# Batch 0 in a new order: sixteen-row loads of the last key and value rows, key sums by pairwise additions, an expert guess on one column

## The chip, the cores and the metric

The kernel runs on one core of a Trainium2 chip. The core has a matrix engine (PE, with its weight loads listed apart as PEld), a vector engine (DVE), a scalar engine (ACT), a general engine (POOL) and a sequencer (SP) that here does little but start DMAs. Each engine runs its own list of instructions in order and waits on semaphores for the others. The metric is the device time of one execution in microseconds (us): the median of the runs.

## The reference, cut to what matters

```python
# attention per batch b (8) and head (8); 576 tokens, head size 64
k_p = k.reshape(B, H, 72, 8, D).mean(axis=3)     # keys and values pooled over 8 rows
v_p = v.reshape(B, H, 72, 8, D).mean(axis=3)
attn = softmax(q @ k_p.T / sqrt(D));  x = attn @ v_p      # x: 4608 tokens x 512
# two-step routing: best of 4 groups, then best of the 4 experts of that group
g_idx = argmax(x @ w_group);  e_idx = argmax(x @ w_expert[g_idx])
out = g_w * e_w * (relu(x @ w1[g_idx, e_idx]) @ w2[g_idx, e_idx])
```

Each token goes through one of 16 experts, with w1 of 512 x 1024 and w2 of 1024 x 512.

## The kernel before, in words

**Stages.** For each batch the kernel has an attention part (class Att) and an expert part (class Moe). The expert part takes all 576 tokens of a batch through one expert, the one that most of its tokens choose ("main expert"); the tokens of other experts are done at the very end by a loop (class Left). While the expert part of batch b runs on PE, the attention of batch b+1 is worked in between its matmuls.

**Batch 0 is special.** Nothing runs beside its attention, and its expert's weights can't be loaded before the expert is known. So the kernel guesses the expert: guess_x and guess_e route the mean of the values, as if each token attended to all keys alike. guess_e ends with a number (tile me) that SP loads into a register, and the loads of the expert's weights (tile sw) take their address from it. Any guess gives a right output, since tokens of other experts go to the loop.

**Names.** u is a half of the heads (0 or 1), c a piece of 128 tokens (the last of 64), g a pair of heads.

- load_k, load_v: 512 KB of keys or values for 128 of the 144 pooled rows of a pair (tile kv). load_r: the other 16 rows of each pair (tile rem), keys in partitions 96 to 127, values in 64 to 95.
- kr, vr, rr: the sums over 8 rows, from kv into kp or vp, and from rem into rp. On DVE it is one reduction; on POOL it is fold, three additions of 512, 256 and 128 elements.
- kb, kt: masks the key sums on ACT and transposes them on PE. qt: transposes a piece of q on PE. sc: scores. mx, sb, su_, nm: maximum, subtraction and exponential, sum and reciprocal, and normalization (nm on DVE with "v", on POOL with "p"). px_, pm: transposed probabilities; pxd, pmd: their low parts. av: attention output, avd: its low part (tile xt). rt, route, count, gates, keep_x: routing and what hangs on it.
- vmain, vrem: value operands for av, partly on POOL.
- m.load m:j loads quarter j of w1 (m=1) or w2 (m=2); m.split makes a high part on ACT (a cast) and a low part on POOL, or on DVE with "v". m.up f:h is twelve matmuls of the first layer (slice f, token half h), which need both parts of quarter f // 2; m.upd its low part on DVE. m.down is the second layer.
- t.warm: matmuls on a constant, whose result nobody reads.

**What sets the order.** The strings START (up to the first m.up), FIRST (batch 0's expert part and batch 1's attention), STEADY and LAST list the pieces; the letters are a for batch 0's attention, n and x for the next two, m for the expert part, w for the next one's. A piece issues all its instructions and DMAs, on whatever engines, at its place. For START all five engines keep the string's order, for FIRST only PE, SP and DVE do; ACT and POOL are then ordered by the framework's scheduler, as are instructions that must wait for a tile to be given up (the loads load_qb of batch 1's q stand later on SP than in the string). Loads are issued by SP, one queue, in order.

Of the kernel before, what the change touches and what calls it, by code (L numbers as in the profile page):

```python
# [46 lines left out]
a.avd:2:256:320 m.split:2:0 n.vr:0 a.av:1:256:320 a.avd:1:256:320 a.av:3:256:320 n.load_v:1 m.load:2:2 n.qb:0 m.up:5:0 a.avd:3:256:320 n.rr
a.rt:256:320 n.kb m.upd:5:0 a.route t.warm:3 m.upd:2:0 x.load_k:0 n.rcopy n.kt m.up:6:0 n.sc:0 m.up:7:0 n.mx:0 n.vr:1:p n.qb:1 n.sb:0
m.up:0:1 m.upd:6:0 n.sc:1 m.upd:7:0 m.split:2:1:p n.su_:0 n.mx:1 n.nm:0:p n.qb:2 m.up:1:1 m.upd:0:1 n.sb:1 a.count n.px_:0 m.up:2:1 a.gates
m.upd:1:1 n.su_:1 n.sc:2 n.nm:1:p x.load_k:1 n.qb:3 n.vmain x.load_r:k x.load_r:v n.pxd:0 n.vrem n.mx:2 m.up:3:1 m.up:4:1 n.px_:1 n.pm:0  # L50
m.upd:2:1 a.keep_x n.sb:2 m.up:5:1 m.load:2:3 n.pmd:0 m.upd:3:1 x.load_qb:3 n.pm:1 x.load_qb:2 n.sc:3 n.pxd:1 n.su_:2 m.upd:5:1 n.pmd:1
m.up:6:1 n.nm:2:p x.load_v:0 m.up:7:1 n.mx:3 n.pm:2 n.sb:3 m.split:2:2:p m.upd:4:1 n.qb:4 n.px_:2 n.sc:4 n.su_:3 m.upd:7:1 n.pxd:2 n.nm:3:p
n.px_:3 n.mx:4 n.pmd:2 n.av:1:0:256 m.split:2:3:p n.sb:4 n.pm:3 m.upd:6:1 n.pxd:3 n.pmd:3 m.down:0 n.su_:4 n.nm:4:p n.av:2:0:256
n.av:0:0:256 m.down:1 n.avd:2:0:256 n.avd:0:0:256 n.avd:1:0:256 n.av:3:0:256 x.load_qb:1 n.px_:4 n.pm:4 n.pxd:4 n.pmd:4 x.kr:0 n.avd:3:0:256
x.load_qb:0 m.down:2 n.av:0:256:320 n.avd:0:256:320 n.rt:0:256 n.av:1:256:320 n.avd:1:256:320 n.av:2:256:320 n.avd:2:256:320 n.av:3:256:320
x.load_v:1 n.avd:3:256:320 x.rr n.rt:256:320 x.qb:1 m.down:3 x.rcopy x.kr:1 n.route m.down:4 x.kb m.down:5 m.down:6 x.qb:0 n.main_expert
m.down:7 n.gates w.load:1:0 m.down:8 x.kt x.vr:1:v w.split:1:0:v m.down:9 x.sc:0 x.vrem x.mx:0 w.load:2:1 w.load:1:1 w.load:1:3 m.down:10
x.sb:0 x.su_:0 w.load:1:2 x.nm:0:v x.vr:0:p m.down:11 n.keep_x m.down:12 x.vmain w.split:1:1:p m.down:13 w.load:2:0
# [817 lines left out]
```

## Time and profile before

| | us |
|---|---|
| median of 3 runs | 615.87 (615.83 to 618.83) |
| the profiled execution | 614.83 |
| its span, first to last instruction | 612.7 |

| engine | busy us | share of the span |
|---|---|---|
| PE | 589.0 | 96% |
| PEld | 525.6 | 86% |
| DVE | 404.8 | 66% |
| ACT | 281.8 | 46% |
| POOL | 253.8 | 41% |

The page cuts the span into 40 slices of some 15.3 us. PE is at 9 tenths in all slices but the first and the third (6 tenths each) and the last (6); the granted PE clock is at full speed but in the first and the fourth slices. DVE is at 8 or 9 tenths in the fifth to the eighth slice. The slices of batch 0 are the first eight or so: the first matmul of its expert part starts at 39.24 us, that of batch 1's at 133.8 us.

Reading the profile: a row of the timeline gives the start and length of one instruction, or of several alike, and in brackets how long the engine stood idle before and what ended the wait. Lengths of matmuls overlap, since PE is pipelined: starts tell more than lengths.

### The profile page before, as it was taken

What the parts mean: (1) busy time and instruction counts of PE and PEld (TensorE: products, weight loads), DVE (VectorE), ACT (ScalarE), POOL (GpSimd) and SP (SyncE); (2) the same over time, 40 slices, a digit from 0 to 9 for tenths busy, and PEclk for the clock granted to TensorE, in tenths of its full rate; (3) what the DMA queues carried; (4) which work ended last, traced back from release to release, by engine and by line L of the source; (5) the groups of instructions that cost most, each with busy time, mean ns of one, the idle gap of its engine ahead of it and who ended that gap; (6) DMA issues with size and microseconds to landing.
All of it is one profiled execution on the core that took longest, in us unless ns stands there. A gap on an engine that the chain in (4) does not pass through costs nothing.

```text
span 612.7 us, 10857 instructions
## 1 busy us (share of the span) xinstructions
PE 589.0 (96%) x3841; PEld 525.6 (86%) x3841; DVE 404.8 (66%) x1000; ACT 281.8 (46%) x585; POOL 253.8 (41%) x255
## 2 busy tenths in 40 slices
PE   6969999999999999999999999999999999999996
PEld 5858887789988999789988998789978998899874
DVE  4886998879774696548774696549673783347231
ACT  3544635366444653555344653455434643243121
POOL 3034546056423663275424663275424662253100
PEclk8998999999999999999999999999999999999999
DMA  6476415255517542454517552484517200541911
GB/s 186 101 243 113 157 36 113 77 200 200 112 52 242 171 83 75 138 186 124 110 49 242 173 88 68 148 347 115 112 39 245 92 1 2 177 176 26 381 68 40
DMA packets 118761, 81.30 MB, mean 133 GB/s; under 512 B 76327, under 2 KB 95271, under 8 KB 118321
## 3 DMA queue, kind: packets, MB, share of 16 engines
q1 hardware_dynamic: 112656, 70.83, 39.4%
q10 hardware_dynamic: 6016, 9.70, 4.4%
q8 instruction: 32, 0.52, 0.4%
q14 instruction: 25, 0.20, 0.1%
q0 software_dynamic: 32, 0.04, 0.0%
HBM read 75.01 MB, written 28.38 MB: 169 GB/s over the span
## 4 chain that ended last, share of the span: by engine, by line
PE 78%; DVE 13%; DMA 3%; ACT 2%; issue 2%; SPq 1%; POOL 0%; DVEq 0%; POOLq 0%
PE mm L532 28%; PE mm L553 26%; PE sc L291 5%; PE tp L358 5%; PE mm L563 5%; DVE kp L208 3%; PE tp L343 2%; DMA kv<-in_v_dram 2%; DMA sw<-in_moe_w_dram 1%; DVE ht L539 1%; PE tp L331 1%; ACT kb L226 1%; PE tp L371 1%; DVE px L320 1%; DVE xt L363 1%
## 5 line engine op out<-in xcount | busy, mean ns | idle before, releaser
L532 PE MATMUL mm<-xt,w 128*128 128x256 f32 (+1 forms) x1536 | 224.5, 301 | 3.8 <-DVE ht L539 1.6
L532 PEld LDWEIGHTS mm<-xt,w 128*128 128x128 f32 x1536 | 208.7, 190 | 7.1 <-issue 1.7
L553 PE MATMUL mm<-w,ht 128*128 128x512 f32 x768 | 187.7, 396 | 0.0
L518 POOL TENSOR_TENSOR w<-sw,w 128x1024 fp32r<-128x1024 f32 x54 | 131.7, 2456 | 95.2 <-ACT w L517 90.9
L553 PEld LDWEIGHTS mm<-w,ht 128*128 128x128 f32 x768 | 140.8, 188 | 29.3 <-issue 0.8
L534 ACT ACTIVATE ht<-mm 128x256 fp32r<-128x256 f32 (+1 forms) x128 | 52.2, 408 | 112.2 <-PE mm L532 110.8
L539 DVE SCALAR_TENSOR_TENSOR ht<-mm,ht 128x256 fp32r<-128x256 f32 (+1 forms) x192 | 60.5, 344 | 35.0 <-ACT ht L534 34.9
L517 ACT CAST w<-sw 128x1024 fp32r<-128x1024 f32 x64 | 65.5, 1048 | 23.2 <-DMA sw<-in_moe_w_dram 13.4
L320 POOL TENSOR_TENSOR px<-p,su 128x96 f32<-128x96 f32 (+1 forms) x72 | 24.5, 360 | 96.3 <-DVE su L312 53.2
L298 DVE TENSOR_REDUCE mx<-sc 128x8 f32<-128x576 f32 (+1 forms) x40 | 29.9, 748 | 36.5 <-PE sc L291 36.5
L291 PE MATMUL sc<-kT,qT 128*128 128x144 f32 (+1 forms) x320 | 47.4, 292 | 0.0
L291 PEld LDWEIGHTS sc<-kT,qT 128*128 128x128 f32 (+1 forms) x320 | 42.6, 184 | 2.3 <-issue 1.6
L324 POOL TENSOR_TENSOR p<-p,su 128x576 f32<-128x576 f32 (+1 forms) x36 | 41.4, 1149 | 2.8
L558 ACT ACTIVATE y<-mm,gm 128x512 f32<-128x512 f32 x32 | 21.9, 684 | 36.8 <-PE mm L553 36.7
L305 ACT ACTIVATE p<-p 128x576 f32<-128x576 f32 (+1 forms) x40 | 27.3, 683 | 21.8 <-DVE p L304 21.7
L310 DVE TENSOR_REDUCE su<-p 128x8 f32<-128x576 f32 (+1 forms) x40 | 29.9, 746 | 8.9 <-ACT p L305 7.9
L569 DVE TENSOR_TENSOR y<-mm,y 64x512 f32<-64x512 f32 x8 | 5.5, 682 | 44.7 <-ACT y L568 44.7
L363 DVE TENSOR_TENSOR xt<-tp,xt 128x320 fp32r<-128x320 f32 (+2 forms) x68 | 29.3, 437 | 7.9 <-ACT xt L359 6.2
L359 ACT CAST xt<-tp 128x320 fp32r<-128x320 f32 (+2 forms) x68 | 26.1, 384 | 17.1 <-PE tp L358 15.1
L208 DVE TENSOR_REDUCE kp<-kv 128x128 f32<-128x1024 f32 x16 | 31.0, 1971 | 2.7 <-DMA kv<-in_k_dram 2.7
L304 DVE TENSOR_TENSOR p<-sc,mx 128x576 f32<-128x576 f32 (+1 forms) x40 | 30.2, 754 | 3.3
L230 POOL TENSOR_TENSOR kv<-kv 128x512 f32<-128x512 f32 x13 | 16.8, 1292 | 32.8 <-DMA kv<-in_v_dram 32.3
(206 smaller groups left out, 739.0 us busy)
## 6 DMA issues: line engine op xcount, KB each, us to landing
sw<-in_moe_w_dram SPq DMA_DIRECT2D x72, 512.0 KB
xscr<-xt SPq DMA_DIRECT2D x8, 2304.0 KB
kv<-in_k_dram SPq DMA_DIRECT2D x16, 512.0 KB
kv<-in_v_dram SPq DMA_DIRECT2D x16, 512.0 KB
out_dram<-y ACTq DMA_DIRECT2D x32, 256.0 KB
q<-in_q_dram SPq DMA_DIRECT2D x112, 72.0 KB
kv<-in_moe_w_dram SPq DMA_DIRECT2D x6, 512.0 KB
ph<-xscr SPq DMA_DIRECT2D x2, 1152.0 KB
```

Of the source, the lines that this page charges most:

```text
L208: red(out=s.kp[:, 2 * u:2 * u + 2, :], in_=s.k[u].rearrange("p g (j d) -> p g d j", j=8), axis=AX.X, op=ALU.add)
L291: nc.tensor.matmul(ps[0:n, g // 2, 144 * (g % 2):144 * (g % 2) + 144], lhsT=s.qT[c][:, g, 0:n], rhs=s.kT[:, g, :], start=(g % 2 == 0), sto ...
L324: eng.tensor_tensor(out=p[0:n], in0=p[0:n], in1=su[0:n].unsqueeze(3).broadcast_to([n, 2, 4, SP]), op=ALU.mult)
L358: nc.tensor.matmul(ps[:, 0:n], lhsT=flat(l[:, g]), rhs=r, start=(i == 0), stop=(i == len(ops) - 1))
L363: tt(out=s.xt[:, 1, g, sl], in0=s.ta[g][:, 0:n], in1=s.xt[:, 0, g, sl].bitcast(F32), op=ALU.subtract)
L517: nc.scalar.copy(out=wh, in_=raw)
L518: (nc.vector if eng == "v" else nc.gpsimd).tensor_tensor(out=wl, in0=raw, in1=wh.bitcast(F32), op=ALU.subtract)
L532: nc.tensor.matmul(ps[:, 0:n], lhsT=l[:, kc, fs], rhs=xt[:, r, kc, sl], start=(kc == 0 and i == 0), stop=(kc == 3 and i == 2))
L534: nc.scalar.activation(out=ht[:, sl], in_=ps[:, 0:n], func=AF.Relu)
L539: stt(out=ht[:, at:at + hi - lo], in0=ps[:, lo - o:hi - o], scalar=0.0, in1=ht[:, lo:hi].bitcast(F32), op0=ALU.max, op1=ALU.subtract)
L553: nc.tensor.matmul(ps, lhsT=s.ht[f][:, 640 * l + o:640 * l + o + 128], rhs=s.w[2, f // 2][r][:, f % 2, :], start=(i == 0), stop=(i == 23))
L563: nc.tensor.matmul(ps, lhsT=s.ht[f][:, 512:640], rhs=s.w[2, f // 2][r][:, f % 2, :], start=(i == 0), stop=(i == 15))
```

## The change

The strings START and FIRST list all pieces of batch 0 in another order. Beside that:

- load_r uses two DMAs of 16 partitions and both halves of the heads, where it used two of 32 partitions and one half each.
- A helper "total" does all the sums: "r" is the reduction on DVE, "v" three additions on DVE, "p" three on POOL. In batch 0 the second key half and the rows of rem are summed by three additions on DVE, both value halves by the reduction; batch 1's second key half goes to POOL, as both its value halves do.
- The first and second halves of batch 0's keys are put into two tiles of pool wp ("w"), so the kv tiles are free for other loads.
- The guess multiplies the value sums by single columns of sel: twelve matmuls with one column, where the columns had been copied 128 times first. The copying (guess) is gone; the one column is spread when it is copied out of PSUM.
- The router's weights (load_wr) are loaded through ACT's queue, no longer SP's.
- 38 matmuls of t.warm are left, of 56: 35 stand before the keys' transposes, none between them and the first m.up.

Of START, its first lines with the loads (the other rows of the strings are moved likewise):

```diff
-a.load_k:0 a.load_k:1 t.warm:6 a.load_r:k a.load_r:v a.rr:0:p a.kr:1 t.warm:1 a.load_q:0 a.load_v:1 t.warm:2 t.warm:1 a.kr:0 a.guess a.rr:96
+a.load_v:0 a.load_k:0:w a.load_k:1:w a.load_r:v a.load_r:k t.warm:16 a.vr:0:r a.kr:0:r t.load_wr a.load_v:1 a.load_q:1 a.load_q:0 a.kr:1:v
...
-            if which == "k":
+            if s.rem is None:
                 s.rem = sk.tile([128, 2, 512], F32, name="rem", bufs=1)
             r, f = (96, k) if which == "k" else (64, v)
-            for z in range(2):
-                nc.sync.dma_start(out=s.rem[r:r + 32, z, :], in_=s.rows(f)[128:144, 2 * z:2 * z + 2, :].rearrange("r g x -> g r x"))
+            for x in range(2):
+                nc.sync.dma_start(out=s.rem[r + 16 * x:r + 16 * x + 16], in_=s.rows(f)[128:144].rearrange("r (z x) c -> x r z c", x=2)[x])
...
+        def total(s, out, a, eng):
+            if eng == "r":
+                red(out=out, in_=a.rearrange("p g (j d) -> p g d j", j=8), axis=AX.X, op=ALU.add)
+                return
+            add = (tt if eng == "v" else nc.gpsimd.tensor_tensor)
+            add(out=a[:, :, 0:256], in0=a[:, :, 0:256], in1=a[:, :, 256:512], op=ALU.add)
+            add(out=a[:, :, 0:128], in0=a[:, :, 0:128], in1=a[:, :, 128:256], op=ALU.add)
+            add(out=out, in0=a[:, :, 0:64], in1=a[:, :, 64:128], op=ALU.add)
...
-                    o = ps[64 * x:64 * x + 64, 128 * g:128 * g + 128]
-                    nc.tensor.matmul(o, lhsT=s.vp[:, g, :], rhs=s.gw[:, x, :], start=True, stop=(x == 0))
+                    nc.tensor.matmul(ps[64 * x:64 * x + 64, g:g + 1], lhsT=s.vp[:, g, :], rhs=sel[:, x:x + 1], start=True, stop=(x == 0))
...
-            nc.scalar.copy(out=s.gx, in_=ps.rearrange("p (g n) -> p g n", g=NG))
+            nc.scalar.copy(out=s.gx, in_=bc(ps[:, 0:NG], 128))
...
-            nc.sync.dma_start(out=wr[:, :, 0:4], in_=wg.rearrange("(c p) e -> p c e", p=128))
+            nc.scalar.dma_start(out=wr[:, :, 0:4], in_=wg.rearrange("(c p) e -> p c e", p=128))
```

Three places show how the order changes on the engines. First SP, behind the load of the guessed expert's number into the register (tile me). Before, in which the four sw loads of w1 are quarters 2, 3, 0 and 1:

```order
L429 ISA x2
L510 ISA
L510 DMA sw<-in_moe_w_dram 128x4x256
L184 DMA rem<-in_v_dram 32x1x512 x2
L510 ISA
L510 DMA sw<-in_moe_w_dram 128x4x256
L172 DMA kv<-in_k_dram 128x2x512
L510 ISA
L510 DMA sw<-in_moe_w_dram 128x4x256
L510 ISA
L510 DMA sw<-in_moe_w_dram 128x4x256
```

And now, in which they are quarters 1, 3, 2 and 0:

```order
L427 ISA x2
L172 DMA kv<-in_k_dram 128x2x512
L503 ISA
L503 DMA sw<-in_moe_w_dram 128x4x256
L503 ISA
L503 DMA sw<-in_moe_w_dram 128x4x256
L503 ISA
L503 DMA sw<-in_moe_w_dram 128x4x256
L176 DMA kv<-in_v_dram 128x2x512
L195 DMA q<-in_q_dram 128x8x64
L503 ISA
L503 DMA sw<-in_moe_w_dram 128x4x256
```

Quarter 0, which the first m.up needs, was the third weight load, behind two small rem loads and one kv load of batch 1; it is now the last, behind batch 1's second key half and first value half and a piece of q.

Second POOL, from the first of its work that is not setup. Before (rem and rp are batch 0's last rows, vp and kp its value sums, w the low part of a quarter, px and p a normalization):

```order
L230 TENSOR_TENSOR rem<-rem 32x2x256
L231 TENSOR_TENSOR rem<-rem 32x2x128
L232 TENSOR_TENSOR rp<-rem 32x128
L246 TENSOR_TENSOR vp<-vp,kp 128x256
L255 TENSOR_TENSOR rp<-rp,rh 32x128
L518 TENSOR_TENSOR w<-sw,w 128x1024 x2
L320 TENSOR_TENSOR px<-p,su 128x96 x2
L324 TENSOR_TENSOR p<-p,su 128x576
```

And now, from the same vmain subtraction on, where both kv are batch 1's:

```order
L244 TENSOR_TENSOR vp<-vp,kp 128x256
L211 TENSOR_TENSOR kv<-kv 128x2x256
L212 TENSOR_TENSOR kv<-kv 128x2x128
L213 TENSOR_TENSOR kp<-kv 128x128
L253 TENSOR_TENSOR rp<-rp,rh 32x128
L211 TENSOR_TENSOR kv<-kv 128x2x256
L212 TENSOR_TENSOR kv<-kv 128x2x128
L213 TENSOR_TENSOR vp<-kv 128x128
L511 TENSOR_TENSOR w<-sw,w 128x1024
L318 TENSOR_TENSOR px<-p,su 128x96 x2
L322 TENSOR_TENSOR p<-p,su 128x576
```

POOL now sums two halves for batch 1 before its first low part, of which one is left in front of the normalizations; that first normalization is piece 2's, which DVE did before.

Third ACT, around the first cast of a weight quarter (w<-sw). Before, with the attention's casts and exponentials for piece 1 and 2 of batch 0 (pr, ph, xt, p):

```order
L359 CAST xt<-tp 128x128 x2
L280 COPY qT<-tp 128x512
L332 CAST pr<-tp 96x2x128
L345 CAST ph<-tp 128x4x128
L359 CAST xt<-tp 128x128 x3
L305 ACTIVATE p<-p 128x576
L359 CAST xt<-tp 128x128
L517 CAST w<-sw 128x1024 x4
```

And now:

```order
L357 CAST xt<-tp 128x128 x2
L510 CAST w<-sw 128x1024
L330 CAST pr<-tp 96x2x128
L343 CAST ph<-tp 128x4x128
L303 ACTIVATE p<-p 128x576
L278 COPY qT<-tp 128x512
L357 CAST xt<-tp 128x128 x4
L510 CAST w<-sw 128x1024 x2
```

The cast of quarter 0 has moved ahead of piece 1's pr and ph and piece 2's exponential.

## Rows read from the trace of the kernel before

**Rows 1.** Windows: busy us by engine (count), granted PE clock, DMA share, GB/s
```profile
39.24:59.34 20.10, 15.27 (x102) 13.21 (x102) 15.95 (x25) 10.42 (x20) 9.46 (x9) 0.83 0.61 140
48.00:52.00 4.00, 4.00 (x19) 3.69 (x18) 1.54 (x4) 1.36 (x4) 1.80 (x3) 0.52 0.58 95
59.34:98.00 38.66, 34.93 (x245) 31.60 (x245) 36.53 (x89) 19.24 (x46) 20.20 (x23) 1.00 0.28 86
134.00:202.00 68.00, 67.91 (x434) 61.14 (x433) 47.51 (x115) 35.05 (x72) 33.49 (x31) 1.00 0.48 140
```
**Rows 2.** Timeline of PE: start, length, line, operation, idle before and releaser
```profile
27.58 0.31 PE L358 MATMUL tp<-ph,vmh 128*128 128x128 f32 x1
...
37.60 1.15 PE L291 MATMUL sc<-kT,qT 128*128 128x144 f32 x8
...
40.50 1.57 PE L532 MATMUL mm<-xt,w 128*128 128x256 f32 x11 [0.87 <-DVE w L518]
43.29 0.32 PE L331 MATMUL tp<-ident,px 128*96 128x128 f32 x1 [1.22 <-DVE px L320]
45.60 0.45 PE L331 MATMUL tp<-ident,px 128*96 128x128 f32 x1 [2.00 <-DVE px L320]
...
48.06 2.92 PE L532 MATMUL mm<-xt,w 128*128 128x256 f32 x12
...
55.18 1.65 PE L532 MATMUL mm<-xt,w 128*128 128x256 f32 x12
...
59.34 0.46 PE L343 MATMUL tp<-ident,p 64*128 64x64 f32 x4 [0.40 <-POOL p L324]
```
**Rows 3.** Timelines of ACT, DVE and POOL around the first weight splits
```profile
38.15 1.04 ACT L517 CAST w<-sw 128x1024 fp32r<-128x1024 f32 x1 [1.36 <-DMA sw<-in_moe_w_dram]
39.22 1.22 DVE L518 TENSOR_TENSOR w<-sw,w 128x1024 fp32r<-128x1024 f32 x1 [1.53 <-ACT w L517]
40.73 4.71 POOL L518 TENSOR_TENSOR w<-sw,w 128x1024 fp32r<-128x1024 f32 x2 [13.51 <-ACT w L517]
41.10 4.45 DVE L320 TENSOR_TENSOR px<-p,su 128x96 f32<-128x96 f32 x2
```
**Rows 4.** Timeline of the first 28 us, key and value sums, guess, softmax
```profile
5.77 3.70 DVE L208 TENSOR_REDUCE kp<-kv 128x128 f32<-128x1024 f32 x2 [2.70 <-DMA kv<-in_k_dram]
...
14.96 3.74 DVE L239 TENSOR_REDUCE vp<-kv 128x128 f32<-128x1024 f32 x2 [3.56 <-DMA kv<-in_v_dram]
...
18.62 0.75 DVE L298 TENSOR_REDUCE mx<-sc 128x8 f32<-128x576 f32 x1
...
18.85 0.44 PE L446 MATMUL tp<-ht,vp 128*64 128x128 f32 x4 [0.30 <-DVE vp L239]
...
21.86 0.58 ACT L449 COPY ht<-tp 128x512 f32<-128x512 f32 x1 [0.99 <-PE tp L448]
...
22.60 0.76 DVE L324 TENSOR_TENSOR p<-p,su 128x576 f32<-128x576 f32 x1
...
23.51 0.96 PE L454 MATMUL tp<-wr,ht 128*128 128x20 f32 x8
...
25.64 0.15 DVE L428 TENSOR_SCALAR me<-ct 128x1 int32<-128x1 f32 x1
...
26.82 0.40 SPq L510 DMA_DIRECT2D sw<-in_moe_w_dram  x1
...
27.24 0.75 DVE L298 TENSOR_REDUCE mx<-sc 128x8 f32<-128x576 f32 x1
```
**Rows 5.** Windows, all engines, for the DMA share and GB/s in the last columns
```profile
4.00:4.50 0.50, 0.50 (x6) 0.50 (x5) 0.00 (x0) 0.26 (x1) 0.44 (x5) 1.00 1.03 393
8.00:8.50 0.50, 0.00 (x0) 0.00 (x0) 0.50 (x1) 0.00 (x0) 0.00 (x0) 1.00 0.14 53
28.00:38.00 10.00, 9.50 (x81) 8.99 (x80) 7.96 (x21) 4.96 (x14) 0.00 (x0) 1.00 0.98 305
```
**Rows 6.** Window of the filler matmuls (t.warm) alone
```profile
27.50:38.80 11.30, 4.21 (x31) 3.58 (x30) 1.00 0.91 285
```

More of the change, by code (lines that the diff above doesn't have):

```diff
@@ new lines @@
+t.warm:19 a.load_q:2 a.load_q:4 n.load_r:k a.rr:v a.kb a.vr:1:r a.kt t.split_wr a.rcopy n.load_r:v a.guess_x a.qt:0 a.guess_e n.load_k:1
+a.sc:0 m.load:1:1 a.vmain m.load:1:3 a.qt:1 a.sc:1 m.load:1:2 a.mx:0 a.sb:0 a.su_:0 a.nm:0:v a.px_:0 a.pm:0 a.mx:1 a.sb:1 a.vrem a.pmd:0
+n.load_v:0 a.su_:1 a.load_q:3 a.pxd:0 a.nm:1:v a.av:0:0:128 a.av:1:0:128 m.load:1:0 a.avd:1:0:128 n.load_k:0 n.load_qb:0 a.avd:0:0:128
+a.qt:2 a.av:3:0:128 a.avd:3:0:128 a.av:2:0:128 a.avd:2:0:128 m.split:1:0:p a.sc:2 a.mx:2 a.px_:1 a.pxd:1 a.pm:1 a.sb:2 a.pmd:1 a.qt:3
@@ L47 @@
[L47 to L58, printed above, removed]
+a.su_:2 a.nm:2:p a.sc:3 a.avd:2:128:128 a.avd:0:128:128 m.up:0:0 a.px_:2 a.pm:2 a.qt:4 a.mx:3 a.sb:3 m.up:1:0 m.load:2:1 a.su_:3 a.sc:4
@@ L59 @@
+m.down:4 m.down:5 m.down:6 n.main_expert x.qb:1 x.kb m.down:7 n.gates x.kt m.down:9 x.rcopy w.load:1:0 w.split:1:0:v w.load:1:1 x.sc:0
+x.mx:0 x.sb:0 x.vrem m.down:10 m.down:12 m.down:8 w.load:2:1 w.load:1:3 w.load:1:2 x.vr:1:p x.su_:0 n.keep_x x.vr:0:r m.down:13
+w.split:1:1:p x.vmain x.nm:0:p m.down:11 w.load:2:0
 """
@@ L163, in __init__ @@
             s.b = b
-            s.xt = s.lt = s.vp = s.kp = s.rp = s.q = None
+            s.xt = s.lt = s.vp = s.kp = s.rp = s.q = s.rem = None
             s.k, s.v, s.qT, s.p, s.px, s.ss, s.su, s.tp, s.ta, s.m = {}, {}, {}, {}, {}, {}, {}, {}, {}, {}
@@ L203, in load_qb, with kr, rr @@
                     nc.sync.dma_start(out=t[r:r + 32], in_=q[s.b, 2 * g + x].rearrange("(j t) (e d) -> e t j d", t=32, e=2)[e])
-        def kr(s, u):
+        def total(s, out, a, eng):
[6 more added lines that the diff above has]
+            add(out=out, in0=a[:, :, 0:64], in1=a[:, :, 64:128], op=ALU.add)
+        def kr(s, u, eng="r"):
             if s.kp is None:
                 s.kp = wk.tile([128, NG, D], F32, name="kp")
-            red(out=s.kp[:, 2 * u:2 * u + 2, :], in_=s.k[u].rearrange("p g (j d) -> p g d j", j=8), axis=AX.X, op=ALU.add)
-        def rr(s, lo=64, eng="v"):
+            s.total(s.kp[:, 2 * u:2 * u + 2, :], s.k[u], eng)
+        def rr(s, eng="r"):
             if s.rp is None:
                 s.rp = wk.tile([128, 2, D], F32, name="rp")
-            if eng == "v":
-                red(out=s.rp[lo:128], in_=s.rem[lo:128].rearrange("p g (j d) -> p g d j", j=8), axis=AX.X, op=ALU.add)
-            else:
-                s.fold(s.rp[64:96], s.rem[64:96])
+            s.total(s.rp[64:128], s.rem[64:128], eng)
         def rcopy(s):
@@ L227, in kb @@
             nc.scalar.mul(out=krz[:, :, 1, :], in_=s.rp[96:128], mul=0.125)
-        def fold(s, out, a):
-            nc.gpsimd.tensor_tensor(out=a[:, :, 0:256], in0=a[:, :, 0:256], in1=a[:, :, 256:512], op=ALU.add)
-            nc.gpsimd.tensor_tensor(out=a[:, :, 0:128], in0=a[:, :, 0:128], in1=a[:, :, 128:256], op=ALU.add)
-            nc.gpsimd.tensor_tensor(out=out, in0=a[:, :, 0:64], in1=a[:, :, 64:128], op=ALU.add)
         def vr(s, u, eng="p"):
@@ L236, in vr @@
                 s.vp = wk.tile([128, NG, D], F32, name="vp")
-            out = s.vp[:, 2 * u:2 * u + 2, :]
-            if eng == "v":
-                red(out=out, in_=s.v[u].rearrange("p g (j d) -> p g d j", j=8), axis=AX.X, op=ALU.add)
-            else:
-                s.fold(out, s.v[u])
+            s.total(s.vp[:, 2 * u:2 * u + 2, :], s.v[u], eng)
         def vmain(s):
@@ L362, in avd @@
             sl = slice(o, o + n)
-            tt(out=s.xt[:, 1, g, sl], in0=s.ta[g][:, 0:n], in1=s.xt[:, 0, g, sl].bitcast(F32), op=ALU.subtract)
+            tt(out=s.xt[:, 1, g, sl], in0=s.ta[g, o][:, 0:n], in1=s.xt[:, 0, g, sl].bitcast(F32), op=ALU.subtract)
         def rt(s, o, n):
@@ L431, in elect @@
             ts(out=s.moh, in0=cr, scalar1=ct, scalar2=None, op0=ALU.is_equal)
-        def guess(s):
-            t = hp.tile([128, 2 * S], F32, name="ht")
-            w, xb = t[:, 0:512].rearrange("p (i n) -> p i n", i=4), t[:, 512:1024].rearrange("p (g n) -> p g n", g=NG)
-            for i in range(4):
-                nc.scalar.activation(out=w[:, i, :], in_=ones, func=AF.Copy, scale=sel[:, i:i + 1])
-            s.gw, s.gx = w, xb
         def guess_x(s):
```

42 lines of the change are left out of this document (24 added, 18 removed).

## The prediction

> **What bounds the kernel now.** I read the page's slices first: PE is full from the fifth slice on. The windows say the same by stage: from 134 to 202 us PE is busy for 67.9 of 68 us, so nothing that is taken off another engine there can pay. Batch 0 is where time is left: between 39.24 and 59.34 PE is busy for 15.3 of 20.1 us, and between 59.34 and 98 for 34.9 of 38.7 [rows 1]. All that the change can win is an earlier arrival at the full stretch, plus these idle times.
>
> Then I read the timeline of the first 60 us in three passes. *Guess:* the first value load lands at 14.96, me is written at 25.79 (25.64 + 0.15), the first weight load starts at 26.82 [rows 4]. *Weights:* ACT stands ready and waits for quarter 0 until 38.15; its low part is done on DVE at 40.44, and the first m.up runs from 40.50 to 42.07 [rows 2, 3]. *Stall:* PE then waits for px twice, until 43.29 and 45.60, because DVE needs 4.45 us for two multiplications of 96 elements while POOL runs two low parts in 4.71 us [rows 2, 3]. After that PE is at its lower level, 1.2 of 2.4 GHz (0.52 from 48 to 52 [rows 1]), and an m.up takes 2.92 us instead of 1.65 [rows 2].
>
> The profiled execution took 614.83 us for a span of 612.7. My sum is made on the span; the median, 615.87, lies 1.04 above the profiled time.
>
> **The change part by part.** *Last rows in 16-row DMAs.* From 8.0 to 8.5 us the DMA share is 0.14 at 53 GB/s, while full windows show 1.03 at 393 [rows 5]: about two of sixteen engines still work. I take it that these carry the 32-row loads, and that value loads queued behind on the same two engines land late for it (first value half 14.96). No row shows a 16-row load; bounds are two engines as now, and all sixteen as in the full window. I take sixteen.
>
> The Trainium skill ("DMA: Bandwidth & Descriptors", section on why a DMA increments its semaphore by 16) says a DMA uses the largest number up to 16 that divides the slowest dimension of both its patterns. By that the old form, which begins with a dimension of 2 on the memory side, gets 2 engines, as the 0.14 suggests, and the new one 16.
>
> With sixteen, the first value half, two key halves, the last rows and the second value half (2.36 MB) take 6.1 us at 393 GB/s; counted from 2.2 us (DVE's first sum starts at 5.77 for 1.05 MB, of which 2.7 us are transfer and some 0.9 the end of it) they land at 8.3 to 10.
>
> *Sums on DVE.* A reduction takes 1.87 us (3.74 for two [rows 4]). Three additions of 512, 256 and 128 elements: 576 elements take 0.76 [rows 4] and 1024 take 1.22 [rows 3], so 1.03 ns per element and 0.69 + 0.43 + 0.30 = 1.42. The first value half should be there at 4.7, halfway between 3.6 (its bytes alone) and 5.77 (two loads, as before), which leaves room for the router's weights on ACT's queue. DVE then runs without a gap: 4.7 + 2 x 1.87 + 2 x 1.42 + 1.87 = 13.15. The pairwise sums save 0.9 us here.
>
> *Guess.* guess_x took 3.0 us (18.85 to 21.86 [rows 4]) with 128 columns. With one column the weight loads stay; between 1.5 and 3.0 I take 2.0. Then the copy 0.58, guess_e 0.96, DVE from there to me 1.32 (24.47 to 25.79) [rows 4], 0.15 of hand-offs: me at 18.15. SP needs 1.03 from me to the first load: 19.2 instead of 26.82. SP has nothing else by then: its rem loads for batch 1 wait for DVE's sum of rem at 11.3 and take four issues.
>
> *Quarter 0* is now the seventh load behind the register, after six of 524 KB and 262 KB in all including itself: 3.4 MB. At the 305 GB/s of 28 to 38 us [rows 5] it is 11.1 us, at 393 it is 8.7. With 1.2 us to the first byte it lands between 29 and 31.5; I take 31. That is 7 us earlier than 38.15.
>
> *Attention then sets the first m.up.* DVE comes out of the guess at 18.4 and starts piece 0's mx at 18.5; before it was 18.62 [rows 4]. So attention starts no earlier: the guess has only moved in front of it. Piece 0's normalization ends at 23.3 (23.36 before). New beside it is POOL's sum of batch 1's keys, at 22.2 as soon as that load lands: three instructions, the first of 512 elements, where a low part has 1024 and takes 2.36 us [rows 3]. [Rows 3] show what a DVE instruction with two inputs in SBUF pays beside POOL: it waits for POOL's to end. I add 1.2 us, between 0 and 2.5. Piece 1's mx then starts at 24.5, not 27.24 [rows 4], and av of piece 0 at 28.2 after two more subtractions, one exponential and one sum (27.58 before).
>
> The Trainium skill ("SBUF — State Buffer", section on the two sides of SBUF) calls that pair of ports an exclusive lock, held for the whole instruction. It agrees with the 4.45 us, and it speaks against handing POOL batch 1's sums while DVE normalizes.
>
> From the first av to the end of sc:3 PE took 11.2 us (27.58 to 38.75 [rows 2]), of which some 3.6 were fillers (31 passes, 4.2 us with overlap [rows 6]). Without them it is 7.6 at full clock. But with no fillers from 15 us on PE is nearly idle between 18.5 and 28, and the idle stretch from 42 to 46 was followed by the lower clock [rows 1, 2]; at 2.92 / 1.65 = 1.77 it is 13.4. I take the middle, 10.5: half the stretch slow. The first m.up then runs from 38.7 to 40.3, not to 42.07: **-1.8 us** (bounds -4.5 and +1.5). ACT reaches quarter 0's cast at about 33, after its landing at 31.
>
> *The stall behind it.* From 42.07 to piece 4's pm at 59.34 it is 17.3 us [rows 2]. The work in it: 15.27 busy [rows 1], less 2.5 for the lower clock (5.7 busy us, 4.0 from 48 to 52 and some 1.7 just before, would be 3.2), less 2.0 for the first m.up: 10.8. Piece 2's normalization now goes to POOL, behind one low part that ended long before, and the other low parts to DVE, so no long POOL instruction stands beside a DVE one; PE comes from a full stretch and should have its full clock. DVE has two low parts there (2.4 us) for the one, less 4.45 + 0.76 for px and p. I add 0.9 for the chain over DVE, ACT and POOL to piece 4: 11.7 instead of 17.3, **-5.5 us** (bounds -6.5 and -2).
>
> *Behind that* DVE sets the pace: 36.5 busy of 38.7 us [rows 1]. It loses one key sum to POOL (1.87) and gets one or two low parts (1.22 each), ahead of the av subtractions that PE's routing waits for. **0** (bounds -2 and +2). From 98 us on nothing changes: PE hides DMAs and sums there.
>
> Sum: -1.8 - 5.5 + 0 = -7.3; span 605.4, that execution 607.5, median by the same shift **608.5 us**.
>
> **Rivals.** *A larger gain.* PE stays at full clock and DVE pays no lock: the first m.up ends at 37.5, and the idle 3.7 us behind 59.34 shrink by half. -4.5 - 6.2 - 1.8 = -12.5, some 603.5. For it: DVE is near empty of work behind 30 us. Against: nothing keeps PE busy from 18.5 to 28.
>
> *The lead is given back.* DVE is 94% busy behind 59.34; it runs two low parts before the av subtractions, and the lock costs 1 to 2 us more in each stretch, since POOL now has normalizations where DVE has low parts. -1 - 3.5 + 1 = -3.5, 612.4.
>
> *The 16-row loads still use two engines.* Then the second value half lands near 14.9, its sum starts there and not at 11.3, and all behind is 3.6 us later: 612.2. It joins the case before in chance.
>
> *Slower: ACT waits for quarter 0.* ACT runs in order, and the cast now stands ahead of piece 1's pr and ph and piece 2's exponential. Every us by which quarter 0 lands behind 33 moves all later attention. 3.4 MB in 20 us is 170 GB/s, between the 53 of two trailing engines and the 393 of all [rows 5]; then it lands at 40.4 and the gain of 7.3 is gone, and from 43.4 on the kernel is slower by more than 0.5%. At 44.5 it is 620.1. Against it: the windows of weight loads show 305, with trailing engines included.
>
> **How the numbers follow.** The forecast (606 to 611.5) has 0.53, the larger gain 0.16, the lead given back and two engines together 0.22, slower 0.06; 0.03 is left for something unseen. 0.5% (3.1 us) is about what a measurement of this kernel tells from no change: faster means below 612.8. Of the 0.22 more than half lies below that: faster 0.53 + 0.16 + 0.12 = 0.81, same 0.10 + 0.03 = 0.13, slower 0.06. The range for 8 in 10 takes in most of both neighbours: 603 to 613.5.
>
> **What would show it.** Right: sw issued at about 19 us; no window of share 0.13 in the first 12 us; quarter 0's cast on ACT with no wait on a DMA; mx of piece 0 near 18.5; half clock somewhere between 20 and 33; the first m.up ending near 40; no DVE px above 1 us behind it; piece 4's pm at about 52; then an unchanged distance from there to batch 1's first m.up (74.5 us, 59.34 to 133.8). Wrong: a DMA wait on ACT behind 33, sw issued behind 22, or a longer distance from piece 4 to batch 1.

## The result and the profile after

| | before | after |
|---|---|---|
| median, us (4 runs each) | 617.11 (615.83 to 618.83) | 610.44 (609.5 to 611.74) |
| ratio | | 0.9895, 95% interval 0.986 to 0.993 |
| profiled execution, its span | 614.83, 612.7 | 609.5, 607.7 |
| first m.up ends | 42.07 | 44.29 |
| from there to piece 4's pm | 17.27 | 10.35 |
| from there to the end of the span | 553.36 | 553.06 |

The kernel is faster by about 1%, and the forecast of 608.5 us was near. The sum under it was not: the first m.up, which should have ended 1.8 us earlier, ended 2.2 us later, and the stall behind it lost 6.9 us where 5.5 were forecast. The last line moved by 0.3 us only. The medians differ by 6.7 us and the two profiled spans by 5.0; the terms below are those of the profiled pair.

The windows of the kernel after answer to [rows 1]; columns as there:

```profile
15.00:38.00 23.00, 18.54 (x83) 16.49 (x84) 12.96 (x32) 9.79 (x22) 8.37 (x9) 0.50 0.69 199
...
44.13:54.64 10.51, 10.31 (x93) 9.52 (x91) 9.03 (x17) 7.28 (x17) 4.37 (x6) 1.00 0.66 108
54.64:98.00 43.36, 40.09 (x278) 36.54 (x279) 40.56 (x103) 23.35 (x54) 20.38 (x23) 1.00 0.42 116
...
134.00:202.00 68.00, 67.93 (x432) 61.06 (x431) 46.74 (x115) 36.00 (x74) 35.06 (x31) 1.00 0.47 139
```

The old stall is gone: behind the first m.up PE is busy for 10.31 of 10.51 us at full clock. Ahead of it stands something new: 23 us at 0.50, half of the full level (1.2 of 2.4 GHz). PE's timeline after, to be held against [rows 2]:

```profile
17.58 1.74 PE L447 MATMUL tp<-wr,ht 128*128 128x20 f32 x8
...
28.99 0.48 PE L356 MATMUL tp<-ph,vmh 128*128 128x128 f32 x1 [0.68 <-ACT ph L343]
31.35 0.44 PE L356 MATMUL tp<-pr,vx 96*128 96x128 f32 x1 [1.17 <-DVE pr L334]
...
35.10 2.23 PE L289 MATMUL sc<-kT,qT 128*128 128x144 f32 x8
...
42.64 1.65 PE L525 MATMUL mm<-xt,w 128*128 128x256 f32 x12
44.13 0.38 PE L329 MATMUL tp<-ident,px 128*96 128x128 f32 x2
...
45.27 1.70 PE L525 MATMUL mm<-xt,w 128*128 128x256 f32 x12
...
54.64 0.43 PE L341 MATMUL tp<-ident,p 64*128 64x64 f32 x4 [0.20 <-ACT lt L370]
```

At half clock guess_e takes 1.74 us instead of 0.96, and sc 2.23 instead of 1.15 (x8 in both). Behind the first m.up px follows with no wait, where 1.22 and 2.00 us were lost.

DVE's timeline after, which answers to [rows 4]:

```profile
4.77 1.94 DVE L208 TENSOR_REDUCE vp<-kv 128x128 f32<-128x1024 f32 x1 [1.70 <-DMA kv<-in_v_dram]
...
11.30 0.69 DVE L211 TENSOR_TENSOR rem<-rem 64x512 f32<-64x512 f32 x1 [1.21 <-DMA rem<-in_k_dram]
12.02 0.42 DVE L212 TENSOR_TENSOR rem<-rem 64x256 f32<-64x256 f32 x1
12.48 0.29 DVE L213 TENSOR_TENSOR rp<-rem 64x128 f32<-64x128 f32 x1
13.52 1.88 DVE L208 TENSOR_REDUCE vp<-kv 128x128 f32<-128x1024 f32 x1 [0.75 <-DMA kv<-in_v_dram]
...
20.47 0.15 DVE L426 TENSOR_SCALAR me<-ct 128x1 int32<-128x1 f32 x1
...
21.45 0.76 DVE L296 TENSOR_REDUCE mx<-sc 128x8 f32<-128x576 f32 x1 [0.69 <-PE sc L289]
...
25.44 1.70 DVE L322 TENSOR_TENSOR p<-p,su 128x576 f32<-128x576 f32 x1
27.07 0.74 DVE L296 TENSOR_REDUCE mx<-sc 128x8 f32<-128x576 f32 x1
...
37.36 0.76 DVE L296 TENSOR_REDUCE mx<-sc 128x8 f32<-128x576 f32 x1 [1.44 <-PE sc L289]
```

The second value half is summed from 13.52, not 11.3. SP's timeline and its waits up to 60 us (the second form: engine and line, what it waited for, us in total, times, longest) say why:

```profile
7.31 0.78 SPq L184 DMA_DIRECT2D rem<-in_k_dram  x2
9.75 0.39 SPq L176 DMA_DIRECT2D kv<-in_v_dram  x1
...
25.04 2.71 SPq L503 DMA_DIRECT2D sw<-in_moe_w_dram  x1
```

```profile
SPq L184 <- DMA wr<-in_moe_w_expert_dram: 2.2, 1, 2.2
...
SPq L184 <- DMA kv<-in_v_dram: 1.8, 1, 1.8
SPq L176 <- DMA wr<-in_moe_w_expert_dram: 1.6, 1, 1.6
```

SP held the last rows and the second value half back for 5.6 us, until older DMAs had landed, the small router loads on ACT's queue among them. Issued at 9.75, the value half could not land at 8.3 to 10. No wait for an older DMA stands ahead of quarter 0's load: it is the seventh that SP issues from 21.49 on, and SP comes to it at 25.04.

### The profile page after: what moved, and what is told of

Same layout as the page of the kernel before. It is cut to its first block, busy times and chain, and to the rows that moved or that the text cites. A ratio compares the mean times of both kernels' runs of the same rounds, so it can differ in the third digit from the quotient of the medians.

```text
span 607.7 us, 10783 instructions
## 1 busy us (share of the span) xinstructions
PE 586.8 (97%) x3805; PEld 525.4 (86%) x3805; DVE 396.4 (65%) x1001; ACT 279.5 (46%) x581; POOL 253.2 (42%) x259
## 4 chain that ended last, share of the span: by engine, by line
PE 82%; DVE 9%; DMA 3%; ACT 2%; SPq 1%; issue 1%; POOL 1%; ACTq 0%; DVEq 0%; POOLq 0%
PE mm L525 30%; PE mm L546 26%; PE sc L289 6%; PE tp L356 6%; PE mm L556 5%; DVE kp L208 3%; PE tp L341 3%; DMA kv<-in_v_dram 1%; PE tp L329 1%; DMA wr<-in_moe_w_expert_dram 1%; SPq L203 1%; DVE ht L532 1%; ACT kb L233 1%; PE tp L369 1%; PE tp L261 1%
## 5 line engine op out<-in xcount | busy, mean ns | idle before, releaser
L546 PE MATMUL mm<-w,ht 128*128 128x512 f32 x768 | 188.0, 396 | 0.0
L511 POOL TENSOR_TENSOR w<-sw,w 128x1024 fp32r<-128x1024 f32 x52 | 126.9, 2457 | 90.4 <-ACT w L510 85.9
L289 PE MATMUL sc<-kT,qT 128*128 128x144 f32 (+1 forms) x320 | 49.6, 301 | 1.0 <-DVE p L302 0.9
L289 PEld LDWEIGHTS sc<-kT,qT 128*128 128x128 f32 (+1 forms) x320 | 44.2, 190 | 3.5 <-ACT qT L278 1.4
L322 POOL TENSOR_TENSOR p<-p,su 128x576 f32<-128x576 f32 (+1 forms) x38 | 43.7, 1149 | 3.0
L211 POOL TENSOR_TENSOR kv<-kv 128x512 f32<-128x512 f32 x14 | 19.2, 1374 | 51.3 <-DMA kv<-in_v_dram 45.7
L556 PE MATMUL mm<-w,ht 128*128 128x512 f32 x128 | 30.5, 389 | 0.0
```

The costliest lines, as they stand in the source:

```text
L289: nc.tensor.matmul(ps[0:n, g // 2, 144 * (g % 2):144 * (g % 2) + 144], lhsT=s.qT[c][:, g, 0:n], rhs=s.kT[:, g, :], start=(g % 2 == 0), sto ...
L322: eng.tensor_tensor(out=p[0:n], in0=p[0:n], in1=su[0:n].unsqueeze(3).broadcast_to([n, 2, 4, SP]), op=ALU.mult)
L511: (nc.vector if eng == "v" else nc.gpsimd).tensor_tensor(out=wl, in0=raw, in1=wh.bitcast(F32), op=ALU.subtract)
L546: nc.tensor.matmul(ps, lhsT=s.ht[f][:, 640 * l + o:640 * l + o + 128], rhs=s.w[2, f // 2][r][:, f % 2, :], start=(i == 0), stop=(i == 23))
L556: nc.tensor.matmul(ps, lhsT=s.ht[f][:, 512:640], rhs=s.w[2, f // 2][r][:, f % 2, :], start=(i == 0), stop=(i == 15))
```

## The experiments

Each kernel was timed in five rounds beside the kernel before (4 to 12 runs of each), in three groups with 16 to 20 runs of the kernel before in each; the changed kernel itself stands with the four runs of the result. Ratios are to before; where intervals overlap, no order is shown. "Letters" are the engine letters of a few pieces, "fillers" constant matmuls (t.warm). In kernels made from before, the first m.up's row is that of its eleven matmuls behind the low part.

| kernel | median | ratio (95%) | first m.up starts | piece 4's pm |
|---|---|---|---|---|
| after | 610.44 | 0.9895 (0.986 to 0.993) | 42.64 | 54.64 |
| before, letters of the change | 611.69 | 0.9932 (0.990 to 0.9965) | 40.72 | 55.03 |
| before, 16-row loads | 614.82 | 0.9972 (0.9946 to 0.9999) | 39.34 | 57.33 |
| after, letters of before | 613.3 | 0.9947 (0.9926 to 0.9969) | 43.20 | 56.58 |
| after, 32-row loads | 612.91 | 0.9932 (0.9906 to 0.9957) | 45.08 | 57.08 |
| after, fillers | 609.42 | 0.9873 (0.984 to 0.9906) | 42.96 | 55.22 |
| after, router's weights through SP | 611.87 | 0.9923 (0.9898 to 0.9948) | 43.18 | 55.18 |
| after, quarter 0 first | 609.9 | 0.99 (0.986 to 0.9939) | 42.64 | 54.64 |
| fillers, quarter 0 first | 609.5 | 0.988 (0.9846 to 0.9914) | 41.81 | 54.47 |
| the same, router through SP, copies first | 611.11 | 0.9918 (0.9889 to 0.9947) | 45.68 | 57.88 |
| after, vrem earlier | 610.16 | 0.9879 (0.9845 to 0.9913) | 42.45 | 54.46 |
| after, vrem, quarter 0, 25 fillers | 608.79 | 0.9856 (0.9819 to 0.9894) | 43.57 | 55.56 |
| the same, 8 more fillers | 610.13 | 0.9879 (0.9844 to 0.9914) | 45.43 | 57.43 |

**The letters alone, put into the kernel before.**

```diff
-m.split:1:1:p
+m.split:1:1:v
-a.nm:2:v
+a.nm:2:p
-m.split:1:2
+m.split:1:2:v
```

> The kernel before with only the sharing of three pieces changed: batch 0's third normalization to POOL, the low parts of w1's quarters 1 and 2 to DVE. Theory: the idle 3.2 us and the lower clock behind the first m.up came from DVE's px waiting for POOL's low parts. Without that PE goes on at full clock; 4 to 5.5 us of 617.1 go, 612. Rival, DVE is full there anyway and two more low parts on it (2.4 us) take the place of the wait: 615.5 to 617.

DVE's and POOL's rows of that kernel, behind its first m.up:

```profile
41.32 1.36 DVE L518 TENSOR_TENSOR w<-sw,w 128x1024 fp32r<-128x1024 f32 x1
...
45.77 1.42 DVE L518 TENSOR_TENSOR w<-sw,w 128x1024 fp32r<-128x1024 f32 x1
```

```profile
40.95 0.65 POOL L320 TENSOR_TENSOR px<-p,su 128x96 f32<-128x96 f32 x2 [13.64 <-DVE su L312]
41.68 2.01 POOL L324 TENSOR_TENSOR p<-p,su 128x576 f32<-128x576 f32 x1
```

The 4.45 us of px are gone [rows 3]; the two engines still meet, but now POOL pays 0.86 (2.01 for an instruction that takes 1.15 elsewhere) and DVE 0.14. Piece 4's pm comes 4.3 us earlier, at 55.03, and the second m.up runs in 1.70 us, at full clock. Three letters give 0.68%, by this figure about two thirds of what the whole change gives.

**The same letters undone in the changed kernel.**

```diff
-m.split:1:0:p  m.split:1:1:v  a.nm:2:p  m.split:1:2:v
+m.split:1:0:v  m.split:1:1:p  a.nm:2:v  m.split:1:2:p
```

> The changed kernel with four letters set back as they stood before: piece 2's normalization and quarter 0's low part on DVE, the low parts of quarters 1 and 2 on POOL. Theory A (the stall came from DVE's px waiting for POOL's low parts, and the lower clock after it): DVE's px behind the first m.up takes over 1 us again, the distance from the first m.up's end to piece 4's pm goes from 10.5 back to 14 to 17 us, median 613.5 to 616.5. Rival B (with the new order the pieces no longer meet, the letters do nothing): distance 10 to 11.5, median 609.5 to 611.5.

The theory was right in kind, and wrong in place and size. DVE's px and p of piece 2 are done by 43.3, before POOL starts, so the order alone already keeps them apart; the wait now falls on another instruction (POOL's row, then DVE's):

```profile
44.70 4.70 POOL L511 TENSOR_TENSOR w<-sw,w 128x1024 fp32r<-128x1024 f32 x2 [8.68 <-ACT w L510]
```

```profile
47.24 2.18 DVE L309 TENSOR_SCALAR su<-su 128x8 f32<-128x8 f32 x1
```

A 0.17 us instruction takes 2.18. From the first m.up's end to piece 4's pm it is 11.4 us, not 14 to 17, and the median lies about 3 us above the changed kernel's. Order and letters each remove most of the stall; their gains don't add.

**16-row loads alone, put into the kernel before, and 32-row loads put back into the changed one.**

```diff
-for z in range(2): dma(rem[r:r + 32, z, :], 32 rows)
+for x in range(2): dma(rem[r + 16*x:r + 16*x + 16], 16 rows)
```

> The kernel before with the 16-row loads of the last rows alone. Theory: the 32-row loads ran on two DMA engines, so the value halves landed at 14.96. With all sixteen they land near 10.5, no window shows a DMA share of 0.13 in the first 15 us, and since DVE waited for nothing else there, the guess and the attention start 3.5 to 4 us earlier; the stall behind the first m.up stays: 617.1 becomes 613.5. Rival, another wait (pieces of q, weights) takes the place of this one: 616 to 617.

> The changed kernel with its last rows loaded by 32-row DMAs again, as before. Theory A (16-row loads matter little here, since the second value half is held by SP's own issue until 9.75 us and the guess by PE's half clock): the value sum of the second half starts within 1.5 us of 13.52, first m.up within 1 us of 42.64, median 609.5 to 612. Rival B (the trailing engines of the old loads hold value and weight loads back): that sum starts behind 15, a window of DMA share under 0.2 stands behind it, the last rows' value sums and first m.up are 2 us or more later, median above 612.

Windows of before with 16-row loads, for the last two columns:

```profile
8.00:8.50 0.50, 0.29 (x3) 0.10 (x1) 0.50 (x1) 0.00 (x0) 0.29 (x1) 1.00 1.02 336
```

At the time at which the old form showed 0.14 and 53 GB/s [rows 5], all engines work; for the engine count the trace agrees with the rule in the Trainium skill ("DMA: Bandwidth & Descriptors", why a DMA increments its semaphore by 16). The value sums start at 12.61 instead of 14.96, but attention is no earlier for it: mx of piece 0 waits for PE's scores, and me stays at 25.66. What is gained, 2.0 us at piece 4's pm, begins with the weights: ACT's cast of quarter 0 starts at 36.98 instead of 38.15, the first m.up 1.2 us earlier. The other 0.8 us come in the stall behind it, where the clock from 46 to 55 us was 0.81 and not 0.67.

In the changed kernel with 32-row loads it is the last rows' sum that is late (DVE):

```profile
14.43 0.69 DVE L211 TENSOR_TENSOR rem<-rem 64x512 f32<-64x512 f32 x1 [4.26 <-DMA rem<-in_k_dram]
...
15.93 1.89 DVE L208 TENSOR_REDUCE vp<-kv 128x128 f32<-128x1024 f32 x1
...
22.89 0.15 DVE L426 TENSOR_SCALAR me<-ct 128x1 int32<-128x1 f32 x1
```

Everything behind is 2.4 us later, to piece 4's pm (57.08). Rival B holds: the 16-row loads are worth about 2.4 us here.

**Fillers in the changed kernel**: 30 constant matmuls in five places, from the keys' transposes to the av of piece 0.

```diff
-a.kt t.split_wr          ... a.sc:0 ... m.load:1:2 a.mx:0 ... a.px_:0 a.pm:0 a.mx:1
+a.kt t.warm:8 t.split_wr ... a.sc:0 t.warm:2 ... m.load:1:2 t.warm:8 a.mx:0 ... a.px_:0 t.warm:4 a.pm:0 t.warm:8 a.mx:1
```

> The changed kernel with 30 filler matmuls put back between batch 0's attention matmuls (8 behind the keys' transposes, 2 behind sc:0, 8 behind sc:1, 4 and 8 around pm:0). Theory: the changed kernel loses 2.1 us at the first m.up because PE is at 1.2 GHz from 15 to 38 us. With fillers the granted clock is 1.00 there, me is written some 1.5 us earlier and the first m.up ends near 40 instead of 44.1: 3 to 4 us less than the changed kernel's 610.4, about 607. Rival 1, DVE sets the pace of batch 0's attention and the clock is hidden behind it: 610.4, the first m.up still near 44. Rival 2, the fillers stand in front of matmuls that others wait for: 611 to 612.

Windows, then PE and ACT of the kernel with fillers:

```profile
12.00:28.00 16.00, 13.79 (x125) 13.06 (x126) 10.02 (x23) 7.48 (x17) 3.38 (x5) 1.00 0.82 219
28.00:36.00 8.00, 4.90 (x39) 4.22 (x38) 4.12 (x12) 3.55 (x9) 2.94 (x5) 1.00 0.81 251
36.00:43.00 7.00, 5.59 (x25) 5.43 (x25) 4.22 (x10) 2.55 (x7) 4.07 (x4) 0.56 0.22 75
```

```profile
31.78 1.19 PE L289 MATMUL sc<-kT,qT 128*128 128x144 f32 x8
...
36.70 0.37 PE L356 MATMUL tp<-ph,vmh 128*128 128x128 f32 x1 [2.57 <-ACT ph L343]
```

```profile
34.80 1.04 ACT L510 CAST w<-sw 128x1024 fp32r<-128x1024 f32 x1 [2.56 <-DMA sw<-in_moe_w_dram]
```

PE has full clock to 36 us, and sc of piece 2 starts at 31.78 instead of 35.10, in 1.19 us instead of 2.23. Then the lead is lost: ACT's cast waits for quarter 0, piece 1's pr and ph stand behind it, PE idles for 2.57 us and is at its lower level again. This is the prediction's slower rival, in small: quarter 0 lands at 34.8 us. In the changed kernel ACT came to the cast only at 35.50, so nothing waited for it there.

**Quarter 0 as the first weight load**, without and with the fillers:

```diff
-a.guess_e n.load_k:1 ... a.av:1:0:128 m.load:1:0
+a.guess_e m.load:1:0 n.load_k:1 ... a.av:1:0:128
```

> The changed kernel with one load moved: weight quarter 0 is the first load behind the expert's register and not the seventh. In the changed kernel ACT's cast of that quarter began at 35.50 us with no wait for a DMA, so theory A (attention's matmuls at half clock set the first m.up) expects nothing: quarter 0 issued near 22.1, its cast still near 35, first m.up between 42 and 43.2 us, median 609 to 611.5. Rival B (quarter 0's late landing already delays the changed kernel through POOL's low part): first m.up below 41 us, median below 608.5.

> The kernel with 30 fillers and quarter 0 loaded first. Theory A: the fillers made attention 4 us earlier up to 33 us, and this lead was lost on ACT, whose cast of quarter 0 (34.80) waited 2.56 us for a load that SP had issued at 25.5 behind six others, with piece 1's pr and ph behind it; PE then idled and fell to half clock from 36 us. With quarter 0 first: its load issued near 21.5, cast near 32.3 with no wait, full clock through 42 us, first m.up between 37.5 and 39.5 us instead of 42.96, median 604.5 to 607. Rival B: PE falls to half clock there anyway, or POOL's low part or another wait takes the cast's place: first m.up above 41.5 us, median within 608 to 611.5 as with fillers alone.

Without fillers the first m.up stays at 42.64, as theory A expected (the ratio is 0.99), but things moved ahead of it. Batch 1's key load now stands behind quarter 0, and POOL sums it from 27.61 and not from 25.14. Piece 0's mx came 0.6 us earlier, its normalization on DVE no longer ran beside that sum (0.76 us, not 1.70), and the first av started at 27.47, 1.5 us earlier. But POOL's subtraction for batch 0's last rows (rp, which vx needs) then stood behind the sum (rows of POOL and PE):

```profile
27.61 1.27 POOL L211 TENSOR_TENSOR kv<-kv 128x512 f32<-128x512 f32 x1 [8.78 <-DMA kv<-in_k_dram]
...
30.38 0.45 POOL L253 TENSOR_TENSOR rp<-rp,rh 32x128 f32<-32x128 f32 x1
```

```profile
31.31 0.47 PE L356 MATMUL tp<-pr,vx 96*128 96x128 f32 x1 [2.64 <-ACT vx L256]
```

The lead was gone there: sc of piece 2 starts at 35.09, as without the edit (35.10). A kernel whose POOL doesn't sum batch 1's keys at this point was not run.

With fillers the cast at 34.80 has no DMA wait any more, but the first m.up doesn't come before 41.81. The windows of this kernel show where the time went:

```profile
18.90:25.60 6.70, 6.03 (x29) 5.62 (x29) 4.93 (x16) 2.65 (x6) 0.54 (x1) 0.54 0.46 159
25.60:40.00 14.40, 11.97 (x97) 11.27 (x97) 9.81 (x25) 7.97 (x19) 7.81 (x9) 0.97 0.66 206
40.00:43.50 3.50, 3.50 (x18) 3.50 (x17) 2.19 (x5) 1.45 (x3) 1.67 (x3) 0.52 0.35 134
```

In this profile PE was at its lower level for some 7 us around the scores (0.54 from 18.9 to 25.6) and again from 40 us, and fillers that ran late stood in front of piece 0's px and av: the first av started near 30.5, 2.7 us later than with fillers alone (27.86). Rival B holds. Up to 25 us PE's list is the same in both kernels, and one profile had 1.00 there, the other 0.54; what decides between them these runs don't show.

**The router's weights through SP's queue**, behind the second value half; then also with the copies of the value sums' last rows ahead of the cast of these weights:

```diff
-t.load_wr a.load_v:1 a.load_q:1 a.load_q:0 ... t.split_wr a.rcopy
+a.load_v:1 a.load_q:0 t.load_wr a.load_q:1 ... a.rcopy t.split_wr
-nc.scalar.dma_start(out=wr[...])
+nc.sync.dma_start(out=wr[...])
```

> The changed kernel with the router's weights issued by SP again, right behind the second value half and a piece of q. Theory: in the changed kernel SP waits 5.6 us in all for earlier DMAs, two of these waits for router weights that ACT issued, before it issues the second value half at 9.75 (landed 13.5). With only SP's own DMAs ahead it is issued near 5 and lands near 10, vr:1 ends near 13.2 instead of 15.4 and everything behind is some 2 us earlier: 608.4. Rival: the router's weights now land too late for guess_e, or the second value half was late for the DMA engines and not for its issue: 610.4 or more.

> As the kernel with fillers and quarter 0 first, and besides SP issues the router's five small loads behind the second value half and the first q load, and ACT issues the copies of the value sums' last rows ahead of the cast of the router's weights. Theory A: taking the router's loads off the early queue gave nothing by itself because that cast then waited 2.98 us for them and the copies stood behind it; with the copies ahead the guess starts at about 14.5 us, me comes between 17.8 and 18.8 instead of 19.87, all behind it is 1 to 2 us earlier than with fillers and quarter 0 alone: median 603 to 606 (0.5 to 2 below that kernel's). Rival B: attention's first piece doesn't hang on the guess (DVE and PE are busy with other things there) or the small loads land later still: me above 19.5 or mx of piece 0 above 19.5, median as the kernel without this edit.

In the first of the two the second value half was summed from 11.62 without a wait, almost where the prediction had it, yet me came at 21.00, later than 20.47. ACT's row shows why:

```profile
15.53 0.26 ACT L810 CAST wrs<-wr 128x80 fp32r<-128x80 f32 x1 [2.98 <-DMA wr<-in_moe_w_expert_dram]
```

The router's weights were then the late ones, with the copies behind them. In the second the copies stood ahead, and now they held the cast: ACT issued the two from 13.51 to 17.58, and the profile puts the cast's wait down to them, not to the weights:

```profile
13.51 4.07 ACTq L228 DMA_DIRECT2D rp<-rp  x2
17.76 0.26 ACT L810 CAST wrs<-wr 128x80 fp32r<-128x80 f32 x1 [4.96 <-DMA rp<-rp]
```

The low part on DVE waited for the cast until 18.05, me came at 21.33, and all behind was later (the profiled run, 614.97 us, is the longest of the nine). Theory A fell both times: the early value half was worth nothing here, since the router's weights and these copies stood in each other's way on ACT.

**Combinations**: vrem's split moved up, first alone, then with quarter 0 first and 25 fillers, then with 8 more fillers ahead of piece 1's av.

```diff
-a.sc:0 m.load:1:1 a.vmain m.load:1:3 ... a.mx:1 a.sb:1 a.vrem
+a.sc:0 m.load:1:1 a.vmain a.vrem m.load:1:3 ... a.mx:1 a.sb:1
```

> The changed kernel with one piece moved: the split of the value sums' last rows (vrem: rh and vx on ACT, rp on POOL) stands behind the split of the other value sums and not behind piece 1's mx. In the changed kernel the last matmuls of piece 0's av waited for it until 31.35 us, 0.9 to 1.2 us after the rest. Theory A: that wait is on the path; vx is written by about 23, PE's gap before 31.35 goes, sc:2 starts 0.9 to 2 us earlier than 35.10, first m.up at 40.8 to 42, median 608 to 609.5. Rival B: vrem's two exponent-free instructions delay ACT's q copy and exponential of piece 0, or PE at half clock sets the pace: first m.up 42.3 to 43.5, median 609.5 to 611.

> The changed kernel with three edits together: vrem moved up, quarter 0 loaded first, and 25 fillers placed where PE waits (8 ahead of the guess, 4 behind piece 0's scores, 7 ahead of its px, 6 ahead of its av). Theory A (half clock, the late cast and vrem together made the first m.up late): PE mostly at full clock to 40 us, no gap over 1 us ahead of sc:2, first m.up at 37.5 to 40.5 us, piece 4's pm at 49 to 52.5, median 604.5 to 608. Rival B (fillers stand in front of real work and cost as much as the clock gains, as in the kernel with 30 fillers and quarter 0 first): first m.up at 41 to 43, median 608.5 to 610.5.

> As the kernel with vrem, quarter 0 first and 25 fillers, and 8 more fillers ahead of the av of piece 1, where PE idled for 1 to 1.5 us and was at half clock from there in the two kernels with 30 fillers. Theory A: the stretch from there to the first m.up keeps full clock (sc:3 in 1.2 and not 1.8 to 2.2 us, m.up in 1.65 and not 1.9 to 2.3), first m.up ends 1 to 1.5 us earlier, median 0.5 to 1.5 below the kernel without them. Rival B: the clock falls all the same, or the eight passes stand in front of av: no gain, median within 0.7 of it or above.

vrem alone gave nothing that can be told. Its premise was wrong: PE waits 1.17 us at 31.16 as it did at 31.35, and for DVE's pr in both. The combination has the lowest median of all, 608.79, but its interval overlaps that of the change, and its profile doesn't show the expected way: PE was at 0.50 from 15 to 20 us again and at 0.55 to 25, me came at 22.47, and the first m.up at 43.57. But this profile is of one of its two longest runs, 610.74 and 611.38 us with a mean granted clock of 0.985. The other four had 0.991 or 0.992 and took 607.13 to 608.9 us, and where PE was slow in these no trace shows. With the 30 fillers alone the four runs stand in the same order: 607.66 us at 0.995 (the theory had 607), and 611.46, the profiled one, at 0.989. With quarter 0 first beside the 30 fillers there is no such order (608.54 to 609.88 at 0.989 to 0.993). So one list of instructions gets different clocks in different runs, and a profile of one run can't refute a theory for the median. The eight more fillers stood in front of av for 2.58 us, and in the profile the first m.up came 1.9 us later; the two intervals overlap.

## Why the prediction was right, and where it was not

That the forecast came within 1.9 us of the median is in part luck: the first m.up missed its forecast by 4.0 us, and the stall gave back 1.4 of them.

**The first m.up (forecast -1.8, measured +2.2).** The step that failed is "10.5, half the stretch slow", from the first av to the first m.up. The stretch took 13.65 us (28.99 to 42.64). That is as long as the prediction's case of half clock throughout (13.4), but it was made of other parts (windows of the changed kernel):

```profile
28.99:38.40 9.41, 8.21 (x35) 7.61 (x36) 5.34 (x14) 4.48 (x11) 5.08 (x5) 0.50 0.65 199
38.40:42.64 4.24, 3.67 (x29) 3.29 (x29) 3.42 (x10) 2.47 (x6) 1.57 (x4) 0.99 0.36 124
```

An estimate from these rows: at the prediction's ratio of 1.77 the 8.21 busy us are 4.64 at full clock, so the clock cost 3.6 us, where the 10.5 had 2.9. The work at full clock is 8.3 us for 7.6. And PE waited for 1.8 us (1.17 of them at 31.35, for DVE's pr), for which the sum had nothing; this is the largest of the three differences. The argument beside the 10.5, a PE nearly idle from 18.5 to 28, doesn't fit either: PE was at 0.50 from about 15 to 38, and at that level its work filled 18.54 of 23 us.

That the clock delays attention is shown as far as sc of piece 2: with fillers it comes 3.3 us earlier. Of these, 0.94 us came about because piece 0's normalization, now at 24.06, started ahead of POOL's key sum (24.51) and took 0.76 us, not 1.70. That the first m.up would be earlier too is not shown: with fillers quarter 0 held ACT, with quarter 0 first the clock and the fillers' place did, and no profile here has both out of the way.

The other 0.8 us of this miss are in the first av's start (28.99 for 28.2), from terms that nearly cancel: the second value half 2.2 late, since SP waited for other DMAs; the guess from that sum to me 5.2 us for 5.0; mx of piece 0 then waited for slow scores, 2.95 behind the forecast in all; and from piece 1's mx to the first av 1.9 us instead of 3.7 (3.1 in the kernel with fillers). The wait in piece 0's normalization beside POOL's key sum was 0.94 us (1.70 for 0.76), for 1.2 forecast.

**The sums on DVE** had the forecast lengths: 0.69, 0.42 and 0.29, first sum at 4.77 for 4.7. **Quarter 0** was forecast for 29 to 31.5; SP issued it only from 25.04, and in the kernel with fillers it landed at 34.8. That ACT's cast had no wait in the changed kernel was right, for a reason that was not in the prediction: ACT was late too. One sign that the prediction had named for being wrong did appear: the first weight load was issued at 22.10, behind 22 and not near 19.

**The stall (forecast -5.5, measured -6.9).** Right in mechanism and in the clock: full throughout, no px above 1 us on DVE. The 0.9 added for the chain to piece 4 was not needed; PE was 98% busy. But the gain has two causes that stand in for each other, the new order and the letters: from the end of the first m.up to piece 4's pm it is 17.3 us in before, 12.7 with the letters alone, 11.4 with the order alone and 10.35 with both.

**Behind piece 4 (forecast 0, measured -0.3).** From its pm to the end of the span it is 552.6 to 555.4 us in the changed kernel and its ten variants, with the pm between 54.5 and 57.9, and no trend between the two. In the two variants of before it is 556.9 and 557.2 (spans of 611.9 and 614.5). One profile stands for each kernel, and it lies up to 3.9 us off the kernel's median, so a few us behind piece 4 can't be told apart there. From piece 4's pm to batch 1's first m.up, forecast as unchanged, it is 73.1 us (54.64 to 127.71) for 74.3 before (59.34 to 133.64).

**Where the 1% comes from.** Put into before, letters and 16-row loads give 0.68% and 0.28%, near the whole 1.05% if they add, which was not run. Undone in the changed kernel they cost 0.52% and 0.37%; these two intervals touch that of the changed kernel, so the sizes are rough. The early guess, which brought the first weight load from 26.82 to 22.10, added little that these runs can tell: the weights then waited for attention.
